# A transformer block on one core: the swapped activations of token tiles 6 and 7 sent earlier, the swapped q and k weights sent later and from another queue

## The chip, the cores and the metric

The kernel runs on one core of a Trainium2 chip. A core has five engines with an instruction stream each: TensorE (PE) for matmuls, VectorE (DVE), ScalarE (ACT) and GpSimd (POOL) for work on elements, and SyncE (SP), which here issues data transfers only. A transfer is issued from the stream of SP or of ACT ("SPq" and "ACTq" in the rows) and is carried out by 16 DMA engines that all queues share. The metric is the device time of one execution in microseconds; smaller is better.

## The reference

The input x has 2048 tokens of 448 features. The kernel computes a normalised x and adds two branches to x:

```python
xn = layernorm(x)
qkv = xn @ wqkv                     # 448 x 1344; 16 heads of 28
s = (q @ k.T) * 28 ** -0.5          # a token sees itself and the 255 before it
o = softmax(s) @ v
out = x + o @ wo + (gelu(xn @ w_gate) * (xn @ w_up)) @ w_down    # 448 -> 1792 -> 448
```

All inputs and the output are bf16.

## The kernel before

**Tiles and blocks.** The 2048 tokens are 16 tiles of 128 and four blocks of 512 (`qb` 0 to 3). Block 0 has tiles 0 to 3, block 1 has tiles 4 to 7. `xnT` holds the normalised x transposed: features on the partitions, in 3 chunks of 128 and one of 64, tokens along the free axis. For tiles 4 and up the transposition is a DMA (`dma_transp`, L184), issued by SP after VectorE has normalised the tile.

**Half arrays and swapped copies.** 448 is 3.5 times 128, so most matmuls work on 64 features at a time, and two of them run side by side, one on partitions 0 to 63 and one on 64 to 127 (the two values of `hi`). Each of the two needs all seven chunks of 64 on its own half of the partitions, so every operand exists a second time with the halves exchanged. `xsw` is the exchanged `xnT` of a block, filled by `swap` (L473 to L479, two transfers for each call); `wvs` is the exchanged v weights; `wsq` is the exchanged q and k weights, filled by `swap_weights` (L481 to L484, two transfers of 192 KB). `wsq` is first read by the q and k projections of block 1 (`qk_pair` in `gen_pairs`, L345). `xsw` of tiles 6 and 7 is read by the v projection of that pair of tiles (`v_pair`, L331).

**The padded weights.** `wqp` and `wkp` hold q and k weights with 28 features of a head in 32 columns. VectorE and ScalarE fill the 28 (`pads`); GpSimd fills the four spare columns with features of other heads (`fill_pads(False)`, L288 to L307, called in `ahead3`). `swap_weights` reads all of it.

**The order of work.** The order is written out by hand: the program text is run once, and each engine gets its instructions in the order in which the text reaches them. Block 0 has eight attention steps. A step writes scores into PSUM (L680), ScalarE takes their exponentials (L685), and then `plan[i]` lists what else is emitted in that step: pieces of other matmul work, such as `(u, 12)`, twelve pieces of the projections, or a function. There is one buffer for scores during attention (`score_pool(1)`, L877), so the scores of a step wait for the exponentials of the step before. In block 0, `plan[2]` calls `ahead3`, which issues almost everything that is loaded later: the swaps, the gate weights `wg`, the rest of the up weights `wu`, the last four tiles of x, the output weights `wo` (eight transfers) and the down weights `wd` (two). All of these go by SP's queue, in that order. `plan[4]` has `(u, 12)` and then `fill_pads(True)`. Steps 6 and 7 hold the pieces of `gen_pairs` for block 1: v of tiles 4 and 5, v of tiles 6 and 7, then q and k. After the attention of a block comes `gated` with the gate and up projections.

**ScalarE as a DMA issuer.** Before the change ScalarE issues one x tile at the start (L87) and three small transfers of block 0 (`o_collect`, L362, called in `hook`).

Of the kernel before, what the change touches and what calls it, by code (L numbers as in the profile page):

```python
# [17 lines left out]
P = 128  # L18
# [9 lines left out]
def kernel(  # L28
# [11 lines left out]
    nc = tc.nc  # L40
# [31 lines left out]
    def rows(w, c0, n):  # L72
        return w[c0 * P:(c0 + n) * P, :].rearrange("(c p) n -> p c n", p=P)

    def load_ffn(dst, w, pairs):

        wv64 = w.rearrange("(c p) (h n) -> p c h n", p=64, h=2)
        ns = slice(pairs.start * P, pairs.stop * P)  # L80
        for hi in range(2):
            nc.sync.dma_start(out=dst[64 * hi:64 * hi + 64, :, ns], in_=wv64[:, :, hi, ns])
# [56 lines left out]
    wsq = const.tile([P, 3, H, 32], bf16, name="wsq")  # L139
# [13 lines left out]
    def stat(t):  # L153
        st = work.tile([P, nc.vector.BN_STATS_DIM], f32, name="st")
        nc.vector.bn_stats(out=st[:, :], in_=x_sb[:, t, :])
        nc.vector.bn_aggr(out=mv_all[:, t, :], in_=st[:, :])
# [8 lines left out]
    def norm(t):  # L165
        xn = work.tile([P, 4, P], bf16, name="xn", bufs=4)
        xf = xn[:, :, :].rearrange("p a b -> p (a b)")
        both = ((0, D, 0), (D, 64, 384))
        for lo, n, src in both if t > 3 else both[:1]:
            nc.vector.tensor_scalar(out=xf[:, lo:lo + n], in0=x_sb[:, t, src:src + n], scalar1=mv_all[:, t, 0:1],  # L170
                                    scalar2=rstd_all[:, t:t + 1], op0=ALU.subtract, op1=ALU.mult)
        xns[t] = xn
# [9 lines left out]
    def dma_transp(t):  # L182

        nc.sync.dma_start_transpose(out=xnT[:, :, t * P:(t + 1) * P], in_=xns.pop(t)[:, :, :].rearrange("p a b -> p (a b)"))  # L184
# [61 lines left out]
    def ring(qb):  # L246

        return slice(qb % 2 * QB, (qb % 2 + 1) * QB)
# [39 lines left out]
    def fill_pads(last):  # L288


        def put(dst, src, n, lo):

            src = src.rearrange("p (j d) -> p j d", d=Dh)[:, :, lo:]
            if n == 4:
                nc.gpsimd.tensor_copy(out=dst[:, 12:16, Dh:32], in_=src[:, :, 24:28])
            src = src[:, :, 0:24].rearrange("p j (g i) -> p g j i", i=8)[:, :, :, 0:4]
            nc.gpsimd.tensor_copy(out=dst[:, 0:12, Dh:32].rearrange("p (g j) i -> p g j i", j=4), in_=src)

        if not last:
            for c in range(3):  # L300
                k = wraw[:, c, D + 12 * Dh:2 * D]
                put(wqp[:, c, :, :], k, 4, 0)
                put(wkp[:, c, :, :], k, 3, 4)
            return
        put(w3p[0:64, :, :], w3k[0:64, :], 4, 0)
        put(w3p[64:128, :, :], w3k[64:128, :], 3, 4)
        nc.gpsimd.memset(w3p[64:128, 12:16, :], 0.0)  # L307
# [165 lines left out]
    def swap(qb, t=None, n=4):  # L473

        t0 = P * (4 * qb if t is None else t)
        to = t0 - qb * QB + ring(qb).start
        for hi in range(2):
            nc.sync.dma_start(out=xsw[64 * hi:64 * hi + 64, :, to:to + n * P],
                              in_=xnT[64 - 64 * hi:P - 64 * hi, 0:3, t0:t0 + n * P])  # L479

    def swap_weights():  # L481

        for hi, src in enumerate((wqp, wkp)):
            nc.sync.dma_start(out=wsq[64 * hi:64 * hi + 64], in_=src[64 - 64 * hi:P - 64 * hi, 0:3])  # L484

    def xchunk(qb, hi, c, t0, n):

# [326 lines left out]
    def ahead3():  # L814
        for t in (5, 6, 7):
            norm(t)
            dma_transp(t)
        swap(1, 4, 2)
        fill_pads(False)
        swap_weights()  # L820
        swap(1, 6, 2)
        load_ffn(wg, B_w_gate, slice(0, 3))
        load_ffn(wg, B_w_gate, slice(3, 7))
        load_ffn(wu, B_w_up, slice(5, 7))
        nc.sync.dma_start(out=x_sb[:, 12:16, :], in_=xv[:, 12:16, :])
        wo_v = A_wo.rearrange("(g j d) n -> j d g n", g=4, j=4)
        tail = A_wo[14 * Dh:, :].rearrange("(t i) n -> i t n", i=4)
        for j, (t0, n) in enumerate(SLOTS):
            nc.sync.dma_start(out=wo[32 * j:32 * j + Dh, 0:n, :], in_=wo_v[j][:, 0:n])
            nc.sync.dma_start(out=wo[32 * j + Dh:32 * j + 32, 0:n, :], in_=tail[:, t0:t0 + n])  # L830
        for k in range(0, NF, 7):
            nc.sync.dma_start(out=wd[:, k:k + 7, :], in_=rows(B_w_down, k, 7))

    for qb in range(NB):
        if qb in (1, 3):
            tc.mark_branch_hint_location("general", hint="LikelyTaken",
                                         engines=[mybir.EngineType.DVE if qb == 1 else mybir.EngineType.PE])
        early = ()
        if qb == 0:
            new_hT(0)  # L840
            early = (0, 1, 2, 3, 4)
            def last_v():
                v_dense(2, pvs[2], False)
                v_copy(2, pvs[2], nc.vector.tensor_copy)

            u = chain(gen_qk(), gen_up(0, (1, 2, 3, 0, 4), (2, 3, 4)))
            w = gen_pairs(1, (("v", 0), ("v", 2), ("k", 0), ("k", 1), ("k", 2)))
            plan = [[last_v, lambda: stat(6), (u, 3), ahead], [(u, 2), ahead2, (u, 2)], [(u, 1), ahead3, (u, 7)], [(u, 8), lambda: stat(8)],
                    [lambda: stat(9), (u, 12), lambda: fill_pads(True)], [(u, 9), "sums"],
                    [(w, 7), "inverse", "scale", (w, 7), lambda: stat(10), (w, 3)],  # L850
                    [(w, 4), lambda: stat(11), lambda: rstd(8, 4), (w, 7), "masks", "sums", (w, 7), "inverse"]]
        else:
            d = gen_down(qb - 1)
            if qb < 3:
                u = gen_pairs(qb + 1, (("v", 0), ("k", 0), ("v", 2), ("k", 1), ("k", 2)))
                plan = [[(d, 14)], [(d, 11)], [(d, 11)], [(u, 7)], [(d, 17)], ["sums", (d, 1), (u, 7), "inverse"], [(u, 11)],
                        [lambda: q_last(qb + 1, nc.vector.tensor_copy), (d, 6), "sums"], [(d, 2), "inverse", (d, 9)],
                        [(u, 9), "masks", (u, 1)]]
                plan[3] = [(d, 1), (u, 7)]
                if qb == 2:  # L860
                    plan[0], plan[2] = [(d, 13)], [(d, 10)]
                if qb == 1:
                    for i, j in enumerate((0, 1, 2, 2)):
                        plan[j].insert(0, lambda t=12 + i: stat(t))
                    plan[4].append(lambda: rstd(12, 4))
                    plan[1] = plan[1][:1] + [lambda: q_last(1, nc.vector.tensor_copy), (d, 8)]
                    plan[2] = plan[2][:2] + [(d, 12), lambda: collect(1)]
                    plan[4].append(lambda: deliver(1))
            else:
                new_hT(3)  # L870
                early = (1, 2, 3, 4, 5, 6)
                u = gen_up(3, early, (4, 5, 6))
                plan = [[(u, 12)], [(u, 9)], [(d, 12)], [(d, 10)], [(d, 12)], [(d, 1), (u, 7), "sums"], [(d, 12), "inverse"],
                        ["sums", "inverse", (d, 11)], [(d, 11)], [(d, 1), "masks", (u, 13), "masks", (u, 1)]]
        if qb in (1, 2):
            swap(qb + 1)
        score_pool(1)  # L877
        rest, after, flush = attention(qb, plan)
        nc.scalar.preload_act_table(ACT.Gelu_apprx_tanh)
        score_pool(2)  # L880
        if qb not in hTs:
            new_hT(qb)

        def hook(f):
            after(f)
            if qb in (1, 2) and f == 0:
                collect(qb + 1)
            if f == (8, 2, 2, 0)[qb]:
                o_collect(qb, nc.sync if qb else nc.scalar)
            if f == (12, 4, 4, 0)[qb]:  # L890
                o_deliver(qb)
                o_finish(qb)
            if qb == 0 and f == 6:
                nc.gpsimd.tensor_copy(out=wo[64:128, 3, :], in_=wo[0:64, 3, :])
            if qb in (1, 2) and f == 10:
                deliver(qb + 1)
            t = ({0: 8, 4: 9, 8: 10, 10: 11} if qb == 0 else {4: 12, 6: 13, 8: 14, 10: 15} if qb == 1 else {}).get(f)
            if t is not None:
                norm(t)
                dma_transp(t)  # L900

        gated(qb, early, rest, flush, hook)
        if qb < NB - 1:
            nc.scalar.preload_act_table_set("natural_log_exp_and_others")
# [159 lines left out]
```

## Time and profile before

| | before |
|---|---|
| median of 3 runs | 212.14 us (211.93 to 212.41) |
| profiled execution | 212.1 us |
| its span, first to last instruction | 210.3 us |
| PE busy | 205.5 us, 98% |
| DVE, ACT, POOL busy | 156.3, 134.6, 43.8 us |

The profile has a page with totals and views of the trace. In a timeline row the first number is the start in us from the start of the span, the second how long the instructions of the row took; then come the engine, the line of the kernel, the operation, what it writes and reads, and how many instructions were merged into the row. A bracket gives the idle time before it and what ended it. In the view of waits a row gives who waited, on what, the total in us, how often, and the longest. In the view by windows a row gives, for one stretch, its length, the busy time of each engine, the granted share of the TensorE clock, the mean busy share of the DMA engines, and GB/s.

### The profile page before, as it was taken

To read this page: it belongs to the slowest core of one execution; us is meant where nothing else is said; L and a number is where in the kernel's file an instruction comes from. 1 tells how busy PE (TensorE), PEld (TensorE's weight loads), DVE (VectorE), ACT (ScalarE), POOL (GpSimd) and SP (SyncE) were. 2 spreads that over 40 slices of the span, in tenths; PEclk is the share of its full clock that TensorE was granted. 3 is DMA by queue.
4 is the path that set the end of the run, shared out by engine and by line. 5 is a ranking of instruction groups with operands and counts; after the bars stand their busy time and mean duration, and the time that the engine had idled before them with its cause. 6 is when DMAs were issued, how large, how long until landed. Compare 5 with 4: busy or idle time off the path is not lost. (4 is left out here: it accounts for less than half of the span.)

```text
span 210.3 us, 6672 instructions
## 1 busy us (share of the span) xinstructions
PE 205.5 (98%) x2842; PEld 98.8 (47%) x2842; DVE 156.3 (74%) x359; ACT 134.6 (64%) x132; POOL 43.8 (21%) x87
## 2 busy tenths in 40 slices
PE   7999999999999999999999999999999999999994
PEld 2444444544454445444445444544444454544572
DVE  6898899899788985696438897395385699596532
ACT  4799896956677977413778788523587787756000
POOL 5389902260000220040000112013000022032000
PEclk9999999999999999999999999999999999999999
DMA  6999989959431001003421000100000010100011
GB/s 171 254 238 230 94 199 223 248 147 254 101 88 42 25 15 28 9 4 67 75 75 47 24 4 24 23 3 20 23 5 0 3 47 3 48 5 16 3 47 50
DMA packets 24890, 15.68 MB, mean 75 GB/s; under 512 B 9208, under 2 KB 24728, under 8 KB 24856
## 3 DMA queue, kind: packets, MB, share of 16 engines
q1 hardware_dynamic: 24614, 15.04, 33.6%
q8 instruction: 23, 0.38, 0.8%
q10 hardware_dynamic: 242, 0.17, 0.3%
q14 instruction: 11, 0.09, 0.2%
HBM read 9.26 MB, written 2.41 MB: 55 GB/s over the span
## 5 line engine op out<-in xcount | busy, mean ns | idle before, releaser
L685 ACT ACTIVATE p_sb<-sc 128x2048 bf16<-128x2048 f32 x38 | 71.4, 1878 | 17.0 <-PE sc L680 12.1
L537 ACT ACTIVATE p_sb<-gt 128x1024 bf16<-128x1024 f32 x28 | 28.6, 1026 | 31.3 <-PE gt L497 30.0
L620 POOL TENSOR_TENSOR oN<-oc,l 128x512 bf16<-128x512 f32 x16 | 20.7, 1301 | 122.4 <-DVE l L633 122.4
L497 PE MATMUL gt<-xnT,wg 64*128 64x512 bf16 x224 | 45.6, 376 | 0.0
L406 PE MATMUL po<-wd,hT 128*128 128x448 bf16 (+1 forms) x224 | 44.7, 347 | 0.0
L497 PE MATMUL gt<-xsw,wg 64*128 64x512 bf16 x168 | 40.7, 376 | 0.0
L605 DVE TENSOR_TENSOR p_sb<-p_sb,masks 128x256 bf16<-128x256 bf16 (+1 forms) x98 | 30.7, 367 | 7.5 <-ACT p_sb L685 7.5
L547 DVE TENSOR_TENSOR hT<-p_sb,u 128x512 bf16<-128x512 bf16 x34 | 21.7, 675 | 13.3 <-PE u L497 13.3
L406 PEld LDWEIGHTS <-hT 128*128 128x128 bf16 x238 | 21.9, 98 | 19.1 <-issue 2.0
L497 PEld LDWEIGHTS <-wg 64*128 64x128 bf16 x392 | 19.0, 94 | 22.3
L497 PEld LDWEIGHTS <-wu 64*128 64x128 bf16 x392 | 19.1, 94 | 22.0 <-issue 0.7
L497 PE MATMUL u<-xnT,wu 64*128 64x512 bf16 x136 | 28.1, 376 | 0.0
L497 PE MATMUL u<-xsw,wu 64*128 64x512 bf16 x102 | 24.7, 376 | 0.0
L497 PE MATMUL ue<-xnT,wu 64*128 64x512 bf16 x88 | 18.1, 377 | 0.0
L639 DVE TENSOR_TENSOR oc<-oc,ov 128x512 f32<-128x512 f32 (+1 forms) x16 | 10.4, 658 | 10.1 <-ACT oc L637 9.9
L497 PE MATMUL ue<-xsw,wu 64*128 64x512 bf16 x66 | 16.2, 377 | 0.0
L680 PE MATMUL sc<-qT,kT 28*64 28x320 bf16 (+4 forms) x736 | 16.2, 259 | 0.0
L394 DVE TENSOR_TENSOR res<-po,x_sb 128x448 bf16<-128x448 f32 (+1 forms) x14 | 8.1, 605 | 7.9 <-PE po L406 6.7
L680 PEld LDWEIGHTS <-kT 28*64 28x64 bf16 x736 | 8.1, 103 | 12.2 <-issue 11.0
L514 DVE CAST hT<-ue 128x512 bf16<-128x512 f32 x16 | 10.6, 686 | 2.0 <-PE ue L497 1.9
L637 ACT COPY oc<-ov 128x512 f32<-128x512 f32 x16 | 9.3, 586 | 3.9 <-PE ov L654 3.8
L633 DVE STREAM_TRANSPOSE l<-inv_all 128x512 f32<-128x512 f32 x16 | 11.1, 700 | 0.1
(112 smaller groups left out, 278.5 us busy)
## 6 DMA issues: line engine op xcount, KB each, us to landing
out_dram<-res SPq DMA_DIRECT2D x15, 112.0 KB
wd<-in_B_w_down_dram SPq DMA_DIRECT2D x2, 784.0 KB
x_sb<-in_A_x_dram SPq DMA_DIRECT2D x3, 448.0 KB
xsw<-xnT SPq DMA_DIRECT2D x6, 192.0 KB
wu<-in_B_w_up_dram SPq DMA_DIRECT2D x4, 224.0 KB
wg<-in_B_w_gate_dram SPq DMA_DIRECT2D x2, 448.0 KB
wu<-in_B_w_up_dram SPq DMA_DIRECT2D x2, 336.0 KB
wg<-in_B_w_gate_dram SPq DMA_DIRECT2D x2, 336.0 KB
```

Of the source, the lines that this page charges most:

```text
L406: nc.tensor.matmul(po[:, 0:w], lhsT=x[:, k, tt * P:(tt + 1) * P], rhs=wt[:, k, lo:up], start=start and n == 0, stop=stop and n == len(term ...
L497: nc.tensor.matmul(ps, lhsT=w[64 * hi:64 * hi + 64, c, p * P:(p + 1) * P], rhs=xchunk(qb, hi, c, qb * QB, QB), start=c == 0, stop=c == 6, ...
L514: copy(out=hTs[qb][:, p + 7 * i, :], in_=us[i])
L537: nc.scalar.activation(out=ges[p][:, :, :], in_=gt[:, :, :], func=ACT.Gelu_apprx_tanh)
L547: nc.vector.tensor_tensor(out=hT[:, p + 7 * i, :], in0=ge[:, i, :], in1=u, op=ALU.mult)
L605: nc.vector.tensor_tensor(out=reg, in0=reg, in1=m, op=ALU.mult)
L620: nc.gpsimd.tensor_tensor(out=oN[:, g, :], in0=oc[:, :], in1=inv, op=ALU.mult)
L633: nc.vector.transpose(out=l1[:, :, :], in_=inv_all[:, 4 * qb + g, :].unsqueeze(2).to_broadcast([P, 16, 32]))
L637: nc.scalar.copy(out=oc[:, :], in_=ov[0][:, :])
L639: nc.vector.tensor_tensor(out=oc[:, q0:], in0=oc[:, q0:], in1=ov[1][:, q0:], op=ALU.add)
L680: nc.tensor.matmul(ss[k0:k0 + nk, j, col:col + nq], lhsT=kT[r, g, kt * P + k0:kt * P + k0 + nk], rhs=qT[r, g, ring(qb).start + q0:ring(qb) ...
L685: nc.scalar.activation(out=p_sb[:, :, 0:ncol], in_=ss[:, :, 0:ncol], func=ACT.Exp, scale=SCALE)
```

## The change

`swap(1, 6, 2)` moves up, directly behind `swap(1, 4, 2)`. `swap_weights` leaves `ahead3` and is called in step 4 of block 0, behind the twelve pieces of `u`; its two transfers are issued by ScalarE instead of SP.

```diff
     def swap_weights():
 
         for hi, src in enumerate((wqp, wkp)):
-            nc.sync.dma_start(out=wsq[64 * hi:64 * hi + 64], in_=src[64 - 64 * hi:P - 64 * hi, 0:3])
+            nc.scalar.dma_start(out=wsq[64 * hi:64 * hi + 64], in_=src[64 - 64 * hi:P - 64 * hi, 0:3])
...
         swap(1, 4, 2)
+        swap(1, 6, 2)
         fill_pads(False)
-        swap_weights()
-        swap(1, 6, 2)
         load_ffn(wg, B_w_gate, slice(0, 3))
...
-                    [lambda: stat(9), (u, 12), lambda: fill_pads(True)], [(u, 9), "sums"],
+                    [lambda: stat(9), (u, 12), swap_weights, lambda: fill_pads(True)], [(u, 9), "sums"],
```

## The prediction

> **What bounds the kernel now.** I read the page's totals first, then the waits, then the timelines of SP, ACT and PE between 24 and 46 us, where the change acts.
>
> ```profile
> span 210.3 us, 6672 instructions
> PE 205.5 (98%) x2842; PEld 98.8 (47%) x2842; DVE 156.3 (74%) x359; ACT 134.6 (64%) x132; POOL 43.8 (21%) x87
> ...
> PEld L331 <- DMA xsw<-xnT: 0.5, 1, 0.5
> ```
>
> TensorE is busy for 98% of the span. What TensorE loses anywhere is lost at the end, and the other engines count only where they make it wait. The profiled execution took 212.1 us, 1.8 more than its span, and the median is 212.14, so the sum can be made against 212.1 and read as the median. The third row is the only wait on a swapped activation: the v projection of tiles 6 and 7 loses 0.5 us. That is all that the earlier swap can win.
>
> The second view is SP's own timeline, the order in which transfers are issued.
>
> ```profile
> 24.57 1.29 SPq L478 DMA_DIRECT2D xsw<-xnT  x2
> 25.96 0.56 SPq L484 DMA_DIRECT2D wsq<-wqp  x1
> 26.62 0.54 SPq L484 DMA_DIRECT2D wsq<-wkp  x1
> 27.25 1.28 SPq L478 DMA_DIRECT2D xsw<-xnT  x2
> 28.58 3.70 SPq L82 DMA_DIRECT2D wg<-in_B_w_gate_dram  x4
> 32.33 1.31 SPq L82 DMA_DIRECT2D wu<-in_B_w_up_dram  x2
> 33.68 0.84 SPq L825 DMA_DIRECT2D x_sb<-in_A_x_dram  x1
> 34.63 2.25 SPq L829 DMA_DIRECT2D wo<-in_A_wo_dram  x1
> 36.92 0.26 SPq L830 DMA_DIRECT2D wo<-in_A_wo_dram  x1
> 37.23 0.32 SPq L829 DMA_DIRECT2D wo<-in_A_wo_dram  x1
> 37.59 0.30 SPq L830 DMA_DIRECT2D wo<-in_A_wo_dram  x1
> 39.30 0.32 SPq L829 DMA_DIRECT2D wo<-in_A_wo_dram  x1
> 40.34 0.25 SPq L830 DMA_DIRECT2D wo<-in_A_wo_dram  x1
> 41.60 0.32 SPq L829 DMA_DIRECT2D wo<-in_A_wo_dram  x1
> 43.53 0.25 SPq L830 DMA_DIRECT2D wo<-in_A_wo_dram  x1
> 43.82 1.00 SPq L832 DMA_DIRECT2D wd<-in_B_w_down_dram  x2
> ```
>
> From 37.9 us on SP no longer issues at once. The view of SP's waits says what it waited for:
>
> ```profile
> SPq L830 <- DMA x_sb<-in_A_x_dram: 1.6, 1, 1.6
> SPq L829 <- DMA wg<-in_B_w_gate_dram: 1.4, 1, 1.4
> SPq L829 <- DMA wu<-in_B_w_up_dram: 1.0, 1, 1.0
> SPq L830 <- DMA wu<-in_B_w_up_dram: 0.7, 1, 0.7
> ```
>
> These waits make no sense by data: a piece of `wo` does not use `wg`, `wu` or x. They do make sense by count. The x load at 33.68 is one transfer. The `wo` issue at 43.53, which waited 1.6 us for it, is the eighth behind it. The issue at 41.60 waited for `wu` and is the eighth behind the second `wu`; the one at 40.34 is the eighth behind the first `wu`; the one at 39.30 is the eighth behind the last `wg`. So transfers take turns at eight completion counters, and **a transfer is not issued before the one eight places ahead of it has landed**. On SP this is harmless: it waits for transfers of its own that are older. The question for the change is what is eight places ahead of `wsq` in its new place.
>
> **The change part by part.**
>
> *The place in the turn.* The turn goes by the program text, since the counters have to be given out when the instruction is written. In the new text `swap_weights` stands in step 4, while `ahead3` with all its transfers stands in step 2. Counting from swap(1, 4, 2): two for tiles 4 and 5, two for 6 and 7, four `wg`, two `wu`, one x, eight `wo`, two `wd`, which makes 21, and the first `wsq` is the 22nd. Eight places ahead is the 14th, the `wo` transfer issued at 37.23; for the second `wsq` it is the one issued at 37.59. ScalarE will stand at its first `wsq` until the third piece of `wo` has landed.
>
> *When ScalarE gets there.*
>
> ```profile
> 24.63 0.59 ACT L514 CAST hT<-ue 128x512 bf16<-128x512 f32 x1
> 25.86 1.88 ACT L685 ACTIVATE p_sb<-sc 128x2048 bf16<-128x2048 f32 x1 [0.64 <-PE sc L680]
> 27.80 0.59 ACT L514 CAST hT<-ue 128x512 bf16<-128x512 f32 x1
> 28.38 0.59 ACT L637 COPY oc<-ov 128x512 f32<-128x512 f32 x1
> 28.87 1.88 ACT L685 ACTIVATE p_sb<-sc 128x2048 bf16<-128x2048 f32 x1
> ```
>
> The cast at 24.63 ends the twelve pieces of step 4; the two issues come behind it, at about 25. Queued behind them on ScalarE is the exponential of step 5, now at 25.86, and all its later work.
>
> *Who waits for ScalarE.* TensorE's timeline:
>
> ```profile
> 27.66 0.62 PE L654 MATMUL ov<-p_sb,v_sb 64*32 64x320 bf16 x36
> 28.21 0.42 PE L680 MATMUL sc<-qT,kT 28*64 28x320 bf16 x16
> ...
> 31.68 0.38 PE L345 MATMUL pk<-xsw,wsq 64*128 64x512 bf16 x1
> ```
>
> The p·v product at 27.66 needs older exponentials only, so TensorE gets to 28.21. There the scores of step 6 need the one score buffer, which the exponential of step 5 has to have read. TensorE stops at 28.2 us.
>
> *When that `wo` piece lands.* No row gives it, so it is bounded. It is behind the x load in SP's queue, and x had landed when the issue at 43.53 went out. The windows:
>
> ```profile
> 41.00:42.00 1.00, 1.00 (x12) 0.49 (x10) 0.96 (x4) 1.00 (x2) 0.00 (x0) 1.00 1.03 230
> 42.00:43.00 1.00, 1.00 (x14) 0.41 (x10) 1.00 (x3) 0.51 (x2) 0.00 (x0) 1.00 0.48 119
> 43.00:44.00 1.00, 1.00 (x12) 0.46 (x10) 0.93 (x4) 0.56 (x1) 0.81 (x1) 1.00 0.13 34
> ```
>
> The DMA engines (second number from the end, 1 is all 16) are full to 42 us, half busy in the next one and at 0.13, two engines out of 16, to 44. So the bulk has arrived at 42.5 and the rest on two late engines by 44. With the change the stream starts a little sooner: the two `wsq` issues leave SP's queue (27.25 less 25.96 is 1.3 us). But swap(1, 6, 2) has to wait for its tiles' transpositions, so it can't use all of that:
>
> ```profile
> SPq L478 <- DMA xnT<-xn: 2.9, 2, 1.6
> ...
> 16.08 6.79 SPq L184 DMA_TRANSPOSE xnT<-xn  x4
> ```
>
> The four transpositions are issued from 16.08 to 22.87. The issue at 24.57 still waited 1.6 us for those of tiles 4 and 5, though the last two issues, for 6 and 7, take about 1.25 us each. Tile 7 should then land near 24.5 + 2 × 1.25, about 27.0 or slightly before, and the stream gains 0.3 to 0.5 us; I take 0.4. The `wo` piece lands between 42.5 - 0.4 = 42.1 and 44.0 - 0.4 = 43.6. I take 42.6, nearer the bulk, since two late engines may be late for reasons that move with the stall.
>
> *ScalarE's issues.* Two at 0.55 us, as on SP (0.56 and 0.54), with nothing between: 1.1 us, bounded by 0 (if they overlap with the engine) and by two times 0.8 (the longest single SP issue without a wait). The exponential starts at 42.6 + 0.05 + 1.1 + 0.1 = 43.85 and takes 1.88: 45.7. Some 0.2 us for the release (in the rows above the scores end at 28.21 + 0.42 = 28.63 and their exponential starts at 28.87): TensorE resumes at 45.95. It stood since 28.2: **17.75 us**.
>
> *Behind the stall.* The cast (27.80) and copy (28.38) run behind the exponential and free the PSUM bank that v of tiles 4 and 5 needs: the cast ends 0.6 us behind the exponential, the scores take 0.4, so +0.2. The 0.5 us wait for `xsw` is gone, since everything has landed long before: -0.5.
>
> *The clock.* TensorE stands still for over 17 us. The rows on that:
>
> ```profile
> 1.41 4.02 PE L150 MATMUL wps<-wo 128*128 128x512 bf16 x9 [1.41 <-DVE wo L124]
> ...
> 8.46 0.82 PE L198 MATMUL s<-xnT,wqp 128*128 128x512 bf16 x3
> ...
> 208.00:211.00 3.00, 0.00 (x0) 0.00 (x0) 0.06 (x1) 0.00 (x0) 0.32 (x1) 0.86 0.20 63
> ```
>
> Nine matmuls at the start take 4.02 us, some 0.43 each. Later three of the same width take 0.82 with the drain of the last, some 0.22 each. So TensorE starts at half speed and reaches full speed after about 4 us of work, and the window from 208 us on, behind the last matmul, has a granted clock of 0.86 on average: it falls back soon after work stops. After 17 us it resumes at half speed. Four microseconds at half speed do the work of two: +2.0, bounds 0 and 3.4. The Trainium skill ("TensorE: Matmul & The Clock Gate", Part 1, "The HAM clock gate") says that the array goes to half rate after an idle window of about 3.4 us and back after about 3.4 us of sustained work, in windows that don't start with the work. By that the loss would be an estimated 1.7 instead of 2.0, and the sum 0.3 us less; the start row, with its 4 us, agrees within the free-running window that the page describes.
>
> *Covered.* `wsq` itself is needed 3.5 us of full-speed work behind the scores (28.21 to 31.68), so near 45.95 + 3.5 + 2.0 = 51.4. It is issued at 42.7 and 43.2, beside the `wd` load:
>
> ```profile
> wd<-in_B_w_down_dram SPq DMA_DIRECT2D x2, 784.0 KB
> ```
>
> At the 230 GB/s of the window from 41 us, those 1.6 MB take 6.8 us. If `wsq` shares the engines with all of it, it lands near 50, which is covered by a little; the upper end of the range allows for no cover. GpSimd's pads move in nothing: POOL is 21% busy. The later loads lose nothing, TensorE being later than before.
>
> *The sum.* 212.1 + 17.75 + 0.2 - 0.5 + 2.0 = 231.55, say **231.5 us**.
>
> **The rivals.**
>
> *No such wait; the change does what it says.* If ScalarE's transfers had counters of their own, ScalarE would spend 1.1 us on issues in a gap of 0.64 us before the exponential of step 5, which has about 0.4 us of slack to the scores at 28.21, and TensorE would lose nothing or a tenth there. `xsw` of tiles 6 and 7 would be sent 0.3 to 0.5 us earlier and the 0.5 us wait would mostly go: 212.1 - 0.4 = 211.7, faster or the same. For it speaks that no row shows ScalarE waiting for a counter: its three issues at L362 were made when old transfers had long landed. Against it: counters given out in the order of the text have no reason to know the queue. This decides in the other direction wherever the transfer eight places ahead lands before 25.8. Chance 0.08.
>
> *A shorter stop.* The turn is as I count it, but the place is another, and `wsq` waits for a `wg` or `wu` piece, issued between 28.6 and 33.0 and landing, by the four waits above, between 33 (nearest row: the 8-deep turn lets SP run without waiting to 37.9) and 41.6. Taking the middle, a release at 37 instead of 42.6: 231.5 - 5.6 = 225.9. Against it stands the count by text, which has one answer. Chance 0.04.
>
> *A second stop.* `wsq` comes behind all of `wd` and lands after 51.4; TensorE then waits again at its first use. With 6.8 us of `wd` ahead of it, and 2.6 us from the issue to the landing of a swap (estimated from the first `xsw` issue at 24.57, whose data the v projection could read without a wait 4 us later), it lands at 43.2 + 6.8 + 2.6 = 52.6 and, with another 0.8 for its own two transfers, costs up to 2 us: 233.5. Chance 0.1, inside the range.
>
> **How the numbers follow.** The long stop has 0.88: 0.78 with a single stop at 231.5, 0.10 with a second. Its own range runs from an early landing and no cold clock (42.1 and 0: 231.5 - 0.5 - 2.0 = 229.0) to a late one with a slow ramp (43.6 and 3.4: 231.5 + 1.0 + 1.4 = 233.9) and, with part of a second stop, 235.0. Outside are the other two cases with 0.12 and what I haven't thought of. A measurement of this kernel tells about 0.2%, 0.4 us, from no change. Slower has 0.92. The first rival's 0.08 lies at the edge of that bound, so 0.05 goes to faster and 0.03 to the same.
>
> **What would show it.** In the changed kernel TensorE's timeline has a hole of some 17 to 19 us that begins at 28.2 us at the scores L680. ACT's timeline has nothing between the cast at 24.63 and two `wsq` issues at 42 to 44, with the exponential behind them. The waits show ScalarE's queue waiting for a transfer of `wo`. The windows show a granted clock below 1 behind the hole, with the projections at 0.43 instead of 0.22. The wait for `xsw` is gone. Wrong it would be if the `wsq` issues stand at about 25 us; and its size is wrong if the hole ends elsewhere than at 46 or the clock stays full.

## The result and the profile after

The changed kernel takes 217.65 us (median of 6 runs, 215.97 to 219.13); the kernel before, on the same chips, 212.03. The ratio is 1.026, with a 95% interval of 1.021 to 1.031: 2.6% slower. The forecast was 231.5 us, with a range of 229 to 235, so the direction was right and the size wrong by a factor of more than three. The profiled execution took 218.17 us. Ratios here and below leave out runs that took over 1.5% more than the fastest run of the same kernel, which bears on one experiment.

The page of the changed kernel, its totals and the two rows of the clock and of PE in forty slices (a digit is tenths):

```profile
span 216.4 us, 6672 instructions
PE 208.4 (96%) x2842; PEld 99.4 (46%) x2842; DVE 156.4 (72%) x359; ACT 134.9 (62%) x132; POOL 43.8 (20%) x87
...
PE   7999939999999999999999999999999999999994
...
PEclk9999985999999999999999999999999999999999
```

The work is the same and the span is 6.1 us longer. PE has a dent in the sixth slice (27 to 32 us); the clock has one in the same slice and a deeper one in the next. The rest of the PE row is as full as before. The timelines of ACT, then of PE, at that place:

```profile
25.21 0.59 ACT L514 CAST hT<-ue 128x512 bf16<-128x512 f32 x1
27.59 0.52 ACTq L484 DMA_DIRECT2D wsq<-wqp  x1
29.79 0.47 ACTq L484 DMA_DIRECT2D wsq<-wkp  x1
30.31 1.88 ACT L685 ACTIVATE p_sb<-sc 128x2048 bf16<-128x2048 f32 x1 [4.50 <-DMA wsq<-wqp]
```

```profile
28.25 0.62 PE L654 MATMUL ov<-p_sb,v_sb 64*32 64x320 bf16 x36
32.24 0.65 PE L680 MATMUL sc<-qT,kT 28*64 28x320 bf16 x16 [3.37 <-ACT p_sb L685]
...
42.85 0.38 PE L497 MATMUL gt<-xnT,wg 64*128 64x512 bf16 x1
```

The forecast hole is there, at the forecast place and by the forecast chain: ScalarE stands in front of its two issues, the exponential of step 5 is queued behind them, and TensorE waits for that exponential at the scores of step 6. But ScalarE is let go at 29.8 us and not at 42.6. The hole is 3.4 us long and not 17.75. The bracket at 30.31 names the first `wsq` transfer as what ended the wait; that is the profile's inference, and by the times recorded at its counter this transfer landed only at 30.7. What did hold the issues is shown below.

The view by windows of the changed kernel (length, then busy time of PE, PEld, DVE, ACT and POOL, granted clock, DMA share, GB/s):

```profile
28.80:32.20 3.40, 0.07 (x12) 0.10 (x1) 1.11 (x3) 1.89 (x2) 0.00 (x0) 0.80 1.03 244
32.20:37.60 5.40, 5.36 (x42) 2.13 (x43) 2.40 (x5) 3.27 (x4) 0.54 (x1) 0.50 1.11 225
37.60:42.00 4.40, 4.40 (x63) 2.03 (x61) 3.81 (x10) 2.41 (x2) 0.73 (x1) 0.99 1.14 249
```

Behind the hole TensorE works for 5.4 us at half clock, which costs 2.7.

The difference of the two profiles by stage comes from the timelines of TensorE. Rows of before, then the scores of step 4 in the changed kernel:

```profile
22.21 0.42 PE L680 MATMUL sc<-qT,kT 28*64 28x320 bf16 x16
...
36.68 0.38 PE L497 MATMUL gt<-xnT,wg 64*128 64x512 bf16 x1
```

```profile
22.79 0.42 PE L680 MATMUL sc<-qT,kT 28*64 28x320 bf16 x16
```

Up to the scores of step 4, where the work is the same, the changed kernel's profile is already 0.58 us later (22.79 instead of 22.21). The profiles of the experiments below have these scores between 22.2 and 23.2, so this is scatter, and the profile of before lies at its lower end. From there to the scores of step 6 it takes 32.24 - 22.79 = 9.45 instead of 6.00: +3.45, the hole. From there to the first gate product it takes 42.85 - 32.24 = 10.61 instead of 8.47 (28.21 to 36.68): +2.14, which is the 2.7 of the clock less the 0.5 us wait for `xsw`, now gone. The rest of the span is 173.55 instead of 173.62. Together 0.58 + 3.45 + 2.14 - 0.07 = 6.10.

### The profile page after: what moved, and what is told of

Its sections match the earlier page's. It is cut to its first block, busy times and chain, and to the rows that moved or that the text cites. A ratio compares the mean times of both kernels' runs of the same rounds, so it can differ in the third digit from the quotient of the medians.

```text
span 216.4 us, 6672 instructions
## 1 busy us (share of the span) xinstructions
PE 208.4 (96%) x2842; PEld 99.4 (46%) x2842; DVE 156.4 (72%) x359; ACT 134.9 (62%) x132; POOL 43.8 (20%) x87
```

## The experiments

The theory after this result: a transfer is held until the one eight turns ahead has landed, as forecast, but the turns are not given out in the order of the text. The trace records with each transfer the counter that it adds to, and when. There are eight counters, used in rotation, and in that rotation the two `wsq` issues of the changed kernel stand among SP's loads: the first between the two `wu` transfers, the second behind them. Eight turns ahead of them stand the second swap of tiles 4 and 5 and the second swap of tiles 6 and 7. By the times recorded at their counters these two landed at 27.51 and 29.72 us; the `wsq` issues went out at 27.59 and 29.79. The data of `wsq` were ready before that: GpSimd's last write to `wkp` ended at 23.7. That the rotation goes by when each engine is expected to get to its instruction is a guess; no run shows what sets it. The rivals: the two issues are held by the traffic on the DMA engines that both queues share, or by the swaps as such; or a large part of the 5.6 us has to do with the second queue and not with ScalarE's delay.

**Two more transfers in between.**

```diff
+        for _ in range(2):
+            nc.sync.dma_start(out=spare_rows.pop(), in_=A_wo[0:16, 0:32])
         load_ffn(wu, B_w_up, slice(5, 7))
...
```

`spare_rows` are two parts of a small tile that nothing reads; the two lines that make them are left out here.

> The changed kernel with two tiny extra transfers (1 KB each, into an unused tile) on SP between the wg and the wu loads. The second wsq issue then stands eight places behind the first wg transfer, which landed near 32.3 us in the changed kernel, instead of behind the second swap of tiles 6 and 7 (29.7 us). Theory: the second wsq issue moves from 29.8 to about 32.4, the hole on TensorE grows from 3.4 to about 6 us, and the time by 2.6, to about 220.2 us; what the cold clock costs stays as it is. Rival (ScalarE is held by traffic on the shared DMA engines, or by the swaps as data): two transfers of 1 KB change nothing, 217.7 us.

Measured 221.17 us (220.70 to 221.57), ratio 1.044 (1.041 to 1.047). ACT's timeline (the line numbers are two higher here):

```profile
27.28 0.52 ACTq L486 DMA_DIRECT2D wsq<-wqp  x1
32.33 0.47 ACTq L486 DMA_DIRECT2D wsq<-wkp  x1
32.84 1.88 ACT L687 ACTIVATE p_sb<-sc 128x2048 bf16<-128x2048 f32 x1 [7.27 <-DMA wg<-in_B_w_gate_dram]
```

One kilobyte more, twice, and the second issue moves from 29.79 to 32.33 us. The bracket names a `wg` transfer, on which `wsq` doesn't depend as data: the first one, eight turns ahead, landed at 32.26. The forecast was 2.6 us more; it is 3.5 against the median of the changed kernel, and 2.8 against 218.36, the median of those of its runs that have the mean clock of all four runs here (0.984).

**Two transfers fewer.**

```diff
-        load_ffn(wg, B_w_gate, slice(0, 3))
-        load_ffn(wg, B_w_gate, slice(3, 7))
+        load_ffn(wg, B_w_gate, slice(0, 7))
```

> The changed kernel with wg loaded in two transfers instead of four, the same bytes. Two transfers fewer stand between the swaps and wsq, so the two wsq issues stand eight places behind the transposition of tile 7 (landed at 26.6 us) and the second swap of tiles 4 and 5 (27.5 us). Theory: the second wsq issue at 27.6 us, the exponential of step 5 at 28.1, a hole on TensorE of about 1.2 us, too short for the clock to fall: about 213.1 us. Rival (traffic, or the swaps as data): the hole stays at 3.4 us and the clock loss with it, 217.7 us.

Measured 216.21 us (214.55 to 217.17), ratio 1.018 (1.013 to 1.023). ACT's and PE's timelines:

```profile
26.18 0.52 ACTq L484 DMA_DIRECT2D wsq<-wqp  x1
28.21 0.47 ACTq L484 DMA_DIRECT2D wsq<-wkp  x1
...
30.65 0.66 PE L680 MATMUL sc<-qT,kT 28*64 28x320 bf16 x16 [2.34 <-ACT p_sb L685]
```

The release moves the other way, as the turns say. The forecast of the time is a miss: the hole is 2.3 us and not 1.2 (the second swap of tiles 4 and 5 landed at 28.14 in this profile and not at 27.5), TensorE waits another 0.7 us at the first use of `wsq`, whose second transfer landed at 36.14, and the profiled execution has a stretch of half clock after all (mean granted clock 0.991). Of the three other runs, two have a mean clock of 0.999 and 1.0 and take 215.78 and 214.55.

**Four transfers fewer, so that no swap holds ScalarE.** In addition to the edit above:

```diff
-        swap(1, 4, 2)
-        swap(1, 6, 2)
+        swap(1, 4, 4)
```

> As the one before, and tiles 4 to 7 are swapped in two transfers instead of four. The two wsq issues then stand eight places behind the transpositions of tiles 4 and 6, which landed at 23.1 and 24.6 us, before ScalarE gets there. Theory: ScalarE issues both at 25.2 to 26.3 us without being held, no hole at the scores of step 6; but the joint swap has to wait for the transposition of tile 7, so the v projection of tiles 4 and 5 waits about 1 us for xsw: about 212.7 us. Rival (the swaps as data, or traffic): ScalarE is still held until the swaps have landed, near 30 us, and the time is 217 us or more.

Measured 215.85 us (215.10 to 216.10), ratio 1.017 (1.014 to 1.020). ACT's timeline, and rows of the waits:

```profile
25.37 0.52 ACTq L484 DMA_DIRECT2D wsq<-wqp  x1
25.62 0.59 ACT L514 CAST hT<-ue 128x512 bf16<-128x512 f32 x1
26.98 0.47 ACTq L484 DMA_DIRECT2D wsq<-wkp  x1
...
PE pv L331 <- DMA xsw<-xnT: 1.4, 1, 1.4
...
PE gt L497 <- DMA wg<-in_B_w_gate_dram: 0.9, 1, 0.9
```

The joint swap is issued at 27.8 us and lands when v of tiles 4 and 5 has waited 1.4 us for it. ScalarE issued both `wsq` before that, so the swaps as data don't hold it. Eight turns ahead of the two issues now stand the transpositions of tiles 4 and 6. The first landed at 24.03, before ScalarE's issue at 25.37; the second landed at 26.91 us and not at 24.6 as expected, and the second issue went out at 26.98. So ScalarE was still held, for 0.8 us. The hole at the scores is all but gone (0.15 us). The time is again more than forecast: the joint `wg` comes late for the first gate products (0.9), and this profile is a microsecond later than that of before at step 4 already. Two of the four runs also have a mean clock of 0.992. So fewer turns all but set ScalarE free, and the larger transfers cost time at other places.

**Earlier and later on ScalarE.**

```diff
-                    [lambda: stat(9), (u, 12), swap_weights, lambda: fill_pads(True)], [(u, 9), "sums"],
+                    [lambda: stat(9), swap_weights, (u, 12), lambda: fill_pads(True)], [(u, 9), "sums"],
```

> The changed kernel with the two wsq issues ahead of the twelve pieces of step 4 instead of behind them. Two transfers fewer are counted between, so wsq stands behind the first and second swap of tiles 4 and 5 (27.2 and 27.5 us). But the cast of step 4 is now queued behind the issues too, and it frees a bank that the up projection needs at about 26 us. Theory: the second issue at 27.6, TensorE stands for 2 us at the up projection and not at the scores, 214.5 us with the chance of a stretch of half clock in it. Rival (held by the swaps of tiles 6 and 7 or by traffic): second issue at 29.8 as in the changed kernel, and 218 us or more.

```diff
-                    [lambda: stat(9), (u, 12), swap_weights, lambda: fill_pads(True)], [(u, 9), "sums"],
+                    [lambda: stat(9), (u, 12), lambda: fill_pads(True)], [(u, 9), swap_weights, "sums"],
```

> The changed kernel with the two wsq issues one step later, behind the nine pieces of step 5. Theory (a transfer's turn follows an order in which the instructions of all engines are merged, so a later place in ScalarE's work stands behind later transfers): the two issues stand behind the third wg transfer (36.7 us in the changed kernel) and the first wu transfer (39.8 to 41.3); ScalarE is free at about 41, the copy that frees the banks for v of tiles 6 and 7 comes behind it, TensorE stands from 30 to 42 us, two stretches of half clock: about 226 us. Rival (ScalarE waits for the swaps, wherever it is): the issues at about 30 us and no more than 218 us.

The earlier place: 215.67 us (214.05 to 216.42), ratio 1.018 (1.015 to 1.021). The later one: 225.76 us (two runs, 224.17 and 227.36), ratio 1.065 (1.047 to 1.083). ACT's timeline of the earlier place:

```profile
26.56 0.52 ACTq L484 DMA_DIRECT2D wsq<-wqp  x1
27.29 0.58 ACTq L484 DMA_DIRECT2D wsq<-wkp  x1
27.92 0.58 ACT L514 CAST hT<-ue 128x512 bf16<-128x512 f32 x1 [2.44 <-DMA xsw<-xnT]
```

and of the later one:

```profile
36.58 0.52 ACTq L484 DMA_DIRECT2D wsq<-wqp  x1
39.64 0.47 ACTq L484 DMA_DIRECT2D wsq<-wkp  x1
40.15 0.59 ACT L637 COPY oc<-ov 128x512 f32<-128x512 f32 x1 [11.33 <-DMA wu<-in_B_w_up_dram]
```

Each time ScalarE is let go when the transfer lands that the turns name: the second swap of tiles 4 and 5 in the one (landed at 27.21 us), the first `wu` load in the other (39.56). Twelve pieces forward in the list bring the release 2.5 us earlier than in the changed kernel, and one step back brings it ten microseconds later. The later place lost what was forecast for it (226). In the earlier one the issues go out as forecast and the hole is at the up projection, 1.4 us long and not 2, but the time is 1.2 us above the forecast: the profiled run (214.05) has full clock, the three others have 0.99.

**The same place, by SP.**

```diff
-            nc.scalar.dma_start(out=wsq[64 * hi:64 * hi + 64], in_=src[64 - 64 * hi:P - 64 * hi, 0:3])
+            nc.sync.dma_start(out=wsq[64 * hi:64 * hi + 64], in_=src[64 - 64 * hi:P - 64 * hi, 0:3])
```

> The changed kernel with the wsq issues in the same place of the text but on SP. They then stand behind all of SP's loads, are issued at about 45 us behind wd, and land near 50. ScalarE isn't held, and there is no hole at the scores of step 6. Theory: TensorE waits at the first use of wsq, from 31 to 50 us, with one or two stretches of half clock: about 233 us. Rival (the place in the text matters little, the queue is what costs): 213 us or less.

Measured 233.27 us (two runs, 232.74 and 233.81), ratio 1.10 (1.094 to 1.107). SP's timeline and a row of the waits:

```profile
43.28 0.53 SPq L484 DMA_DIRECT2D wsq<-wqp  x1
43.92 0.56 SPq L484 DMA_DIRECT2D wsq<-wkp  x1
...
PE pk L345 <- DMA wsq<-wkp: 18.9, 1, 18.9
```

On SP the place in the text is the place in the queue, behind all loads. It is the place in the rotation too: by their counters the two issues are the 22nd and 23rd transfers from the first swap, as the prediction counted. From the same place in the text, but on ScalarE, they are the 10th and 12th. So the text alone doesn't set the turn. The loss has the size that the prediction expected of the changed kernel, by another path: TensorE waits for `wsq` itself and not for ScalarE.

**Only ScalarE's delay, with no transfer moved.** To the kernel before, with `hold` in the place of `swap_weights` in step 4:

```diff
+    idle = const.tile([P, 192], bf16, name="idle")
+
+    def hold():
+        for _ in range(13):
+            nc.scalar.copy(out=idle[:, :], in_=wvs[:, 0, 0:192])
...
```

> The kernel before, with no transfer moved, and thirteen copies of 192 columns into an unused tile on ScalarE at the place where the changed kernel has the two wsq issues; some 0.3 us each, 3.9 us in all, of which about 1 us is idle or slack. Theory (the loss is ScalarE's delay at this place, and the clock that falls after the hole; queues and traffic have no part): a hole of about 2.9 us at the scores of step 6, one or two stretches of half clock worth 1.7 us each, about 217 us, like the changed kernel. Rival (a large part of the loss comes from the second queue's traffic): the hole alone, about 214.5 us.

and the same with `range(8)`:

> As the one before with eight copies, 2.4 us: a hole of about 1.3 us. Theory (the clock falls only when about half of a stretch of 3.4 us is idle): the clock stays full, 212.9 us. Rival (any hole of a microsecond costs a stretch of half clock): 214.6 us and a mean granted clock of 0.992.

Thirteen copies: 217.75 us (216.88 to 218.47), ratio 1.028 (1.025 to 1.031), the time of the changed kernel. Eight copies: 214.86 us (213.64 to 215.66), ratio 1.011 (1.008 to 1.015). Rows of the thirteen, ACT's timeline, PE's, and a window:

```profile
25.27 4.97 ACT L838 COPY idle<-wvs 128x192 bf16<-128x192 bf16 x13
...
32.06 0.65 PE L680 MATMUL sc<-qT,kT 28*64 28x320 bf16 x16 [3.61 <-ACT p_sb L685]
...
32.00:35.20 3.20, 3.14 (x30) 1.25 (x31) 1.16 (x3) 2.75 (x4) 0.00 (x0) 0.50 1.12 220
```

A hole of 3.6 us from copies alone, with the half clock behind it, costs what the change costs. The runs agree clock by clock too: 217.07 us with the copies against 217.05 with the change where the mean clock is 0.992, and 218.36 against 218.36 where it is 0.984. So the second queue has no large part in the 5.6 us; a part of up to about a microsecond, the scatter of runs at one clock, is not excluded. A copy took 0.38 us and not the 0.3 expected, so the eight made a hole of 1.7 us and not 1.3. Two of their four runs have full clock and take 213.64 and 214.17, two have 0.992 and take 215.56 and 215.66. So neither expectation held for all of them, and as the hole was longer than the one they were made for, the case doesn't decide between them.

**The earlier swap alone, on SP.** To the kernel before:

```diff
         swap(1, 4, 2)
+        swap(1, 6, 2)
         fill_pads(False)
         swap_weights()
-        swap(1, 6, 2)
```

> Only the order on SP is changed: the swap of tiles 6 and 7 directly behind that of 4 and 5, then the swapped weights, still on SP. Theory (ScalarE is held by the turn of the completion counters, and that alone is the loss): no hole on TensorE at 28 us, the 0.5 us wait for xsw shrinks to 0.1 or less, 211.7 us, 0.2% under the kernel before. Rival (the early swap itself does harm, by colliding with other transfers): slower than before by more than 1 us.

This missed: 213.69 us over eight runs (212.03 to 215.46). The ratio, without the two runs at 215.35 and 215.46, is 1.005 (1.002 to 1.008), so about 1 us slower where 0.3 faster was expected. That is at the edge of the rival, harm by the early swap itself. SP's and PE's timelines of the profiled run, the slowest of the eight:

```profile
24.65 3.63 SPq L478 DMA_DIRECT2D xsw<-xnT  x4
28.33 0.60 SPq L484 DMA_DIRECT2D wsq<-wqp  x1
29.03 0.55 SPq L484 DMA_DIRECT2D wsq<-wkp  x1
...
33.47 0.39 PE L345 MATMUL pk<-xsw,wsq 64*128 64x512 bf16 x1 [1.58 <-DMA wsq<-wkp]
```

The swap of tiles 6 and 7 waits for the transposition of tile 7, and `wsq` behind it is issued 2.4 us later than before (28.33 instead of 25.96). In this profile it lands after its first use and TensorE waits. How much of this wait the faster runs have, no profile shows. It suggests that the early swap needs `wsq` out of its way, since SP issues one behind the other.

**The swapped weights first, on SP.** To the kernel before:

```diff
-        swap(1, 4, 2)
         fill_pads(False)
         swap_weights()
+        swap(1, 4, 2)
         swap(1, 6, 2)
```

> The kernel before with the pads and the swapped weights on SP ahead of both swaps, and the two swaps in a row. SP stands idle from 22.9 to 24.6 us, waiting for the transposition of tile 5; GpSimd's pads are ready at 23.3, so the two wsq issues fit into that wait and delay neither the swap of tiles 4 and 5 nor, by more than the wait for tile 7, that of 6 and 7 (from 27.25 to about 26.8). Theory (both operands can be early if neither queues behind a late one): no hole, the wait for xsw falls from 0.5 us to 0.1, 211.7 us. Rival (the bytes of wsq, some 1.5 us of all DMA engines, push the first swap past 28.6 us): a wait of up to 0.7 us there, 212.3 us.

SP's timeline:

```profile
23.34 0.50 SPq L484 DMA_DIRECT2D wsq<-wqp  x1
23.95 0.54 SPq L484 DMA_DIRECT2D wsq<-wkp  x1
24.59 3.15 SPq L478 DMA_DIRECT2D xsw<-xnT  x4
```

The weights go out in SP's wait for tile 5 and delay nothing; the wait for `xsw` is gone from TensorE, and there is no hole. From the scores of step 6 to the first gate product it takes 36.55 - 28.54 = 8.01 us instead of 8.47. The time is 212.0 us in 12 runs against 212.17, ratio 1.0001 (0.9985 to 1.0017): the interval reaches to a gain of 0.3 us, so the 0.46 us that the profile shows at this stage are not confirmed by the times. Of all the versions this is the only one that shows no loss.

## Why the prediction was wrong

*The bound, and the wait to be won (right).* TensorE's 98% and the 0.5 us wait for `xsw` were the right frame: each stop of TensorE went through to the end, and the wait is gone.

*The eight turns (right).* Held behind a transfer without any common data, ScalarE's issues moved by the count in five kernels, in each within 0.1 us of the landing eight turns ahead wherever they were held: with two transfers more or fewer between, with four fewer, and with an earlier or later place. That ScalarE's issues take part in SP's turns, the ground on which the first rival stood with 0.08, is settled with it.

*The place in the turn (wrong; the step that failed).* "The turn goes by the program text" was argued from how instructions are written, and no row was quoted for it. SP's rows could not have tested it, since for one queue alone the text and the order in time are the same. By the counters `wsq` stands 10th and 12th from the first swap, and not 22nd and 23rd; issued by SP from the same place in the text it does stand 22nd and 23rd. What sets the turn of another engine's transfer beyond that stays open. Hence the release at 29.8 instead of 42.6, and a hole of 3.4 instead of 17.75. The rival "a shorter stop", with 0.04, was the case that came, and its own price (release at 37, 225.9 us) was wrong for the same reason: it assumed a `wg` or `wu` piece ahead, and it was a swap.

*Who waits for ScalarE (right).* The hole begins behind the p·v product and is ended by the exponential of step 5, as the chain said; thirteen copies in the same place have the same effect.

*Two issues at 0.55 (right in size).* 0.52 and 0.47, but not one behind the other: each waits for its own turn, and the second, at 29.79, set the end.

*Behind the stall (not seen).* The 0.2 for the bank of v doesn't show: 8.47 - 0.5 + 2.7 = 10.67 already covers the 10.61 us from the scores to the first gate product.

*The clock (mis-sized).* Forecast 2.0, bounds 0 and 3.4. Measured 2.7 in the profile, with 5.4 us of work at half clock. The runs of the changed kernel have a mean clock of 0.992 or 0.984, with medians of 217.05 and 218.36 us: the loss varies between runs. By the rule of the Trainium skill that the prediction quoted ("TensorE: Matmul & The Clock Gate", Part 1), the loss would be an estimated 1.7; the runs show about one or two losses of that size (below).

With the measured hole in the place of 17.75 and without the 0.2, the same sum gives 212.1 + 3.45 - 0.5 + 2.0 = 217.05, or 217.75 with the measured clock term.

## What to carry to other kernels

A transfer issued from a compute engine can be held by the completion counter it shares with older transfers of another queue, and everything behind it on that engine is held with it. Before such a move, find out which transfer is eight turns ahead and when it lands, from the counters that a trace shows and not from the text; and put the issue where the engine has nothing urgent behind it, or leave it on a queue that does nothing else. A short hole on the busiest engine costs more than its length when the clock falls behind it.

## What was not expected of the hardware

The clock falls after holes much shorter than the 17 us of the prediction, and what it loses comes in steps. What a run lost is its span times the part of the clock that was not granted. The changed kernel lost (1 - 0.992) × 215.4 = 1.7 us of clock in three runs and (1 - 0.984) × 216.4 = 3.5 in the other three; the thirteen copies gave 0.992 twice and 0.984 twice. Of the 3.5 in the profile, 0.7 fell into the hole itself (a clock of 0.80 over 3.4 us) and cost nothing. A loss of 1.7 is 3.4 us at half rate, one stretch of the length that the Trainium skill states for the window ("TensorE: Matmul & The Clock Gate", Part 1). The traces agree: in their clock records the half rate lasts 3.41 us in the kernel with eight copies (30.87 to 34.28) and twice that, 6.83, in the changed kernel (30.84 to 37.66). Two windows of the kernel with eight copies show such a stretch behind a hole of only 1.7 us:

```profile
28.60:30.30 1.70, 0.04 (x7) 0.07 (x1) 1.08 (x3) 1.70 (x2) 0.00 (x0) 1.00 0.64 140
30.30:34.30 4.00, 3.97 (x37) 3.00 (x38) 2.09 (x5) 3.25 (x4) 0.00 (x0) 0.57 1.13 241
```

In the hole the clock is full; it is half in most of the four microseconds of work that follow. In the earlier-place kernel a hole of 1.4 us left the profiled run at full clock, while its three other runs have 0.99. The Trainium skill speaks on that page of an idle window of about 3.4 us; here a hole of half that length was enough in some runs and not in others. Whether this depends on where the hole lies in a window that runs by itself, as the Trainium skill would have it, none of these runs was made to decide, but the clock records of the profiled ones speak for it. In them the clock changes only at multiples of 3.41 us from its first rise. Counted in these divisions, the eight copies have 1.69 us of idle TensorE in the one ahead of the fall. The hole of the changed kernel lies across two, with 1.97 and 1.40, and two divisions of half rate follow; that of the thirteen copies lies almost whole in one, with 3.34, and one follows. The earlier place has 1.38 in one division, and the clock stays. So the same hole can cost one stretch, two or none. Where the limit lies is not shown: in the later-place kernel a division with 0.54 of idle, at half rate, was followed by half rate too.
